# Two sliding-window attention layers between Fourier layers, on one core: exponents and scores take turns in five PSUM banks

## The chip, the cores and the metric

The kernel runs on one core of a Trainium2 chip. The metric is the device time of one execution in microseconds (us). A core has five engines with a queue each: TensorE (PE, with its weight loads shown as PEld), VectorE (DVE), ScalarE (ACT), GpSimd (POOL) and SyncE (SP), which here only issues DMAs. An engine works through its queue in order; it waits on semaphores for the others.

## The reference

```python
def _A_ref(x, wqkv, wo):                      # x: 1 x 2048 x 576
    H = 32; Dh = D // H; W = 256              # 32 heads of 18
    q, k, v = ...                             # from x @ wqkv
    scores = einsum("bhqd,bhkd->bhqk", q, k) * (Dh ** -0.5)
    mask = (0 <= idx[:, None] - idx[None, :]) & (idx[:, None] - idx[None, :] < W)
    p = softmax(where(mask, scores, -1e9))
    return einsum("bhqk,bhkd->bhqd", p, v) ... @ wo

x = A_x
x = x + _A_ref(layernorm(x), A_wqkv, A_wo)
x = x + _B_ref(layernorm(x), B_w_r, B_w_i)    # rfft2, times weights, irfft2
x = x + _A_ref(layernorm(x), A_wqkv, A_wo)
x = x + _B_ref(layernorm(x), B_w_r, B_w_i)
```

The change is in `_A_ref`, which is run twice.

## The kernel before

The program is written as one order of instructions by hand; each engine gets its instructions in that order. `layer_a` normalises and transposes the 2048 tokens, projects v, and then does attention; `layer_b` follows. All of this happens twice ("the first and the second layer" below).

Attention goes by *units*. A unit t is one tile of 128 tokens for four heads: there are 8 groups of four heads (`NQ`) and 16 tiles (`NT`), so 128 units (`NX`). The four heads are two pairs; the heads of a pair lie in the upper and lower 64 rows of the array, `hp` 0 and 1, and their matmuls run side by side.

For each unit there are two kinds of scores:

- `score_max` (S, L790 and L792) runs ten units ahead (`LEAD`). PE multiplies q by k for one tile of queries and up to 384 keys into a PSUM tile `S`; VectorE adds the mask and takes the maximum of each row into `m`. After four units, `m_rows` (L798 to L805) transposes the maxima on PE (`tpm`), ScalarE negates them (`mt`), and four DMAs on SyncE put them as a row into `qs`, so that the second multiplication subtracts them.
- `exps` (E, L822 and L823) multiplies the other way round, keys by up to 384 queries, into a PSUM tile `E`; ScalarE writes the exponent of it into `P` in SBUF, which has five buffers, one a unit. GpSimd masks `P`.

`pv` (U, L842) multiplies the exponents of the two or three tiles that matter with v, two units later, and adds up in the bank `U`. Every fourth unit ScalarE copies the sums out (`us`, L847), and `norm` transposes them (`tpo`, L852) and divides on VectorE.

Between these stand the projections to q and k (`proj`, `pj`, L741): 28 blocks of 14 steps for the groups of heads that come later, a few steps in each unit by the table `goal`. When a block's last step is done, ScalarE copies one half's sum into a buffer `sg` (L747), VectorE adds the other half (L748), GpSimd splits the result into two parts (L749, L750), and SyncE stores it into `qk_d` in DRAM (L755). `stack_load` (L769) fetches it back into `qs` and `ks`. The buffer `sg` has two copies. Units -10 to -1 have no E and no U, only S and projections; five blocks end there.

PSUM has eight banks. One is `U`, two are `pj`, three are the tag `S` (scores for maxima, `tpm`, `tpo`), and two are the tag `E` (scores for exponents). In units 118 to 123, which have no S, the second pair's E take the tag `S`. A tile of a tag with n banks waits until the reader of the tile n before it in that tag is done.

The body of a unit, in the order in which it is written:

```python
for pair in range(2):
    for hp in range(2):
        if 0 <= t < NX:
            exps(t, pair, hp)
    for hp in range(2):
        if t + LEAD < NX:
            score_max(t + LEAD, pair, hp)
    if pair == 0 and 0 <= t - 2 < NX:
        pv(t - 2)
    ...                       # for t < 2: half of the unit's projection steps
for f in more:                # the projection steps, then m_rows or norm if due
    f()
```

So PE's queue in a unit reads E E, S S, U, E E, S S, projections, and in two of four units a transposition.

Of the kernel before, what the change touches and what calls it, by code (L numbers as in the profile page):

```python
# [8 lines left out]
F32 = mybir.dt.float32  # L9
F32R = mybir.dt.float32r  # L10
# [5 lines left out]
S, D = 2048, 576  # L16
# [564 lines left out]
def layer_a(tc, src, dst, wqk_d, wv_d, wo_d, dc_d, gc_d, dram, copy, wvs, second, spectral):  # L581
    nc = tc.nc
    V, A, T, P = nc.vector, nc.scalar, nc.tensor, nc.gpsimd
    SC = float(DH) ** -0.5
    qk_d = dram.tile([2, 1152, S], F32R, name="qk_d")
# [5 lines left out]
    with ExitStack() as ctx:  # L591
# [115 lines left out]
        with ExitStack() as c2:  # L707
            wp = c2.enter_context(tc.tile_pool(name="a2", bufs=2))
            pp = c2.enter_context(tc.tile_pool(name="a2p", bufs=2, space=PSUM))
# [16 lines left out]
            def proj(i, c, tag, halves=False):  # L726

                box = {}
                ks = k_steps()
                cs = slice(c * 512, c * 512 + 512)  # L730
                parts = [slice(0, 64), slice(64, 128)] if halves else [slice(0, 128)]

                def mm(s, k):
                    wk, p, xk = k
                    if s == 7 and c == 2 and 0 < i < 8:
                        w_split(i + 1)
                    if s == 0:
                        box["ps"] = [pp.tile([128, 512], F32, tag=tag, name=f"pj{i}_{c}_{b}", bufs=2) for b in range(len(parts))]
                    w = wt[i][0] if p == "h" else wt[i][1]
                    for ps, r in zip(box["ps"], parts):  # L740
                        T.matmul(ps, w[r, wk], xT(xk, cs)[r], start=s == 0, stop=s == len(ks) - 1)  # L741
                    if s == len(ks) - 1:
                        ps = box["ps"]
                        sg = wp.tile([128, 2, 512], F32R, tag="sg", name=f"sg{i}_{c}", bufs=2)
                        if halves:
                            su = sg[:, 1].bitcast(F32)
                            A.copy(su, ps[0])  # L747
                            V.tensor_add(su, su, ps[1])  # L748
                            P.tensor_copy(sg[:, 0], su)  # L749
                            P.tensor_sub(sg[:, 1], su, sg[:, 0].bitcast(F32))  # L750
                        else:
                            A.copy(sg[:, 0], ps[0])
                            V.tensor_sub(sg[:, 1], ps[0], sg[:, 0].bitcast(F32))

                        (nc.scalar if i < 2 else nc.sync).dma_start(qk_d[:, 128 * i:128 * i + 128, cs].rearrange("a r t -> r a t").bitcast(F32), sg.bitcast(F32))  # L755
                return [lambda s=s, k=k: mm(s, k) for s, k in enumerate(ks)]

            vts = {}

# [19 lines left out]
            def score_max(x, pair, hp):  # L779

                n, i = divmod(x, NT)
                c, t = divmod(i, 4)
                q, k = qs[n % 2], ks_[n % 2]
                if t == hp == pair == 0:
                    ms[n, c] = wp.tile([128, 2, 2, 4], F32, tag="m", name=f"m{n}_{c}", bufs=3)
                lo, hi = max(0, i - 2) * 128, (i + 1) * 128
                N = hi - lo
                b = 64 * hp
                ps = pp.tile([128, 512], F32, tag="S", name=f"S{x}_{pair}_{hp}", bufs=3)
                T.matmul(ps[:, 0:N], q[b:b + 63, pair, i * 128:i * 128 + 128], k[b:b + 63, pair, lo:hi], start=True, stop=True)  # L790
                jk = wp.tile([128, 384], BF, tag="jk", name=f"jk{x}_{pair}_{hp}", bufs=3)
                V.tensor_tensor_reduce(out=jk[:, 0:N], in0=ps[:, 0:N], in1=mask[:, 384 - N:384], scale=1.0, scalar=-3e38,  # L792
                                       op0=ALU.add, op1=ALU.max, accum_out=ms[n, c][:, hp, pair, t:t + 1])

            def m_rows(n, c):
                q = qs[n % 2]
                tp = pp.tile([128, 4, 128], F32, tag="S", name=f"tpm{n}_{c}", bufs=3)
                T.transpose(tp[0:16, 0], ms[n, c].rearrange("p a b t -> p (a b t)"), ident)  # L798
                mt = wp.tile([16, 128], F32R, tag="mt", name=f"mt{n}_{c}", bufs=2)
                A.activation(mt, tp[0:16, 0], AF.Copy, scale=-1.0)  # L800
                for hp in range(2):
                    for pair in range(2):
                        r = (hp * 2 + pair) * 4
                        b = 64 * hp + 63
                        nc.sync.dma_start(q[b:b + 1, pair, c * 512:c * 512 + 512].rearrange("a (t q) -> a t q", t=4).bitcast(F32),  # L805
                                          mt[r:r + 4].bitcast(F32))
# [3 lines left out]
            def exps(x, pair, hp):  # L810

                n, j = divmod(x, NT)
                q, k = qs[n % 2], ks_[n % 2]
                nq = min(3, NT - j) * 128
                hl_ = 2 * hp + pair
                if hp == pair == 0:
                    pt[n, j] = wp.tile([128, 4, 384], F32, tag="P", name=f"P{n}_{j}", bufs=5)
                p = pt[n, j]

                ps = pp.tile([128, 512], F32, name=f"E{x}_{hl_}", **(dict(tag="S", bufs=3) if pair and NX - LEAD <= x < NX - 4 else dict(tag="E", bufs=2)))  # L820
                b = 64 * hp
                T.matmul(ps[:, 0:nq], k[b:b + 64, pair, j * 128:j * 128 + 128], q[b:b + 64, pair, j * 128:j * 128 + nq], start=True, stop=True)  # L822
                A.activation(p[:, hl_, 0:nq], ps[:, 0:nq], AF.Exp, scale=SC)  # L823
                if hp == pair == 1:
                    P.affine_select(out=p[:, :, 0:128], in_=p[:, :, 0:128], pattern=[[0, 4], [1, 128]], compare_op=ALU.is_ge,  # L825
                                    fill=0.0, base=0, channel_multiplier=-1)
                    if nq == 384:
                        P.affine_select(out=p[:, :, 256:384], in_=p[:, :, 256:384], pattern=[[0, 4], [-1, 128]], compare_op=ALU.is_gt,  # L828
                                        fill=0.0, base=0, channel_multiplier=1)
# [17 lines left out]
                    A.copy(u, U)  # L847

            def norm(n, c):
                tp = pp.tile([128, 4, 128], F32, tag="S", name=f"tpo{n}_{c}", bufs=3)  # L850
                for a in range(4):
                    T.transpose(tp[:, a], us[n, c][:, a * 128:a * 128 + 128], ident)  # L852
                tv = tp.rearrange("p a (h e) -> p (a h) e", e=32)
                rc = wp.tile([128, 16, 1], F32, tag="rc", name=f"rc{n}_{c}", bufs=2)
                V.reciprocal(rc, tv[:, :, 18:19])
                o = wp.tile([128, 4, 72], F32, tag="o", name=f"o{n}_{c}", bufs=2)
                V.tensor_mul(o.rearrange("p a (h e) -> p (a h) e", e=18), tv[:, :, 0:18], rc.to_broadcast([128, 16, 18]))
                lo, hi = 72 * n, 72 * n + 72
                for a, f0, f1 in ((o_d, 0, 448), (o7_d, 448, 576)):
                    b, e = max(lo, f0), min(hi, f1)  # L860
                    if b < e:
                        nc.sync.dma_start(a[c * 512:(c + 1) * 512, b - f0:e - f0].rearrange("(a p) e -> p a e", a=4), o[:, :, b - lo:e - lo])
# [10 lines left out]
            NX = NQ * NT  # L873
            LEAD = 10
# [4 lines left out]
            for m in range(22):  # L879
                a, b = [2 + 23 * z // 5 for z in (m, m + 1)]  # L880
# [6 lines left out]
            for t in range(-LEAD, NX + 2):  # L887
# [3 lines left out]
                n, c = divmod(t + 20, NT)  # L891
# [10 lines left out]
# [4 lines that stand above are left out]
                    for hp in range(2):  # L906
                        if t + LEAD < NX:
                            score_max(t + LEAD, pair, hp)
                    if pair == 0 and 0 <= t - 2 < NX:
                        pv(t - 2)  # L910
                    if pair == 0 and t < 2:
                        for f in more[:(len(more) + 1) // 2]:
                            f()
                        more = more[(len(more) + 1) // 2:]
                for f in more:
                    f()
                if copy and t >= 32 and t % 4 == 0 and t < 32 + 16 * len(copy):

                    z, r = divmod(t // 4 - 8, 4)
# [36 lines left out]
            for k in range(4):  # L956
                tp = pp.tile([128, 512], F32, tag="E" if k in (1, 2) else "pj", name=f"tpz{k}", bufs=2)[0:32]
# [9 lines left out]
            tp = pp.tile([128, 512], F32, tag="pj", name="tpl", bufs=2)  # L967
# [47 lines left out]
```

## Time and profile before

| | us |
|---|---|
| median of 3 runs | 1584.82 (1583.24 to 1590.53) |
| the profiled execution, and its span | 1586.13, 1584.4 |
| PE, DVE, ACT, POOL busy in the span | 1452.4, 944.0, 823.8, 753.4 |
| exponents on ScalarE (L823), 1024 times | 427.8 |
| maxima on VectorE (L792), 1024 times | 499.5 |
| attention's units -10 to 127, first layer | 106.8 to 511.7 |
| the same, second layer | 898.6 to 1303.0 |

The profile is of one execution. A row of the time line has a start, a length, the engine, the line, the tile written and the tile read, the shape, and a count where equal rows were put together; in square brackets stands the idle time before it and who ended it. Matmuls overlap and their lengths include their way through the array, so on PE the distance from start to start is the measure, not the length.

### The profile page before, as it was taken

The numbers are of one execution on the slowest core, as the hardware profiler recorded it, in microseconds if no ns is written. First come the engines' busy times: TensorE is split into PE (matmuls) and PEld (weight loads), VectorE is DVE, ScalarE is ACT, GpSimd is POOL, SyncE is SP. The second block draws the span as 40 slices with busy tenths as digits, with TensorE's granted clock in tenths as the row PEclk, the third lists the DMA queues.
The fourth block names the chain that finished last, engine by engine and source line by source line (L and its number), as shares of the span: only waits on it lengthen the run. The fifth ranks groups of instructions, "written<-read, shape, count | busy, mean of one in ns | idle before, by whom it ended". The sixth has DMA issues, their size and how long they took to land. (4 is left out here: it accounts for less than half of the span.)

```text
span 1584.4 us, 35203 instructions
## 1 busy us (share of the span) xinstructions
PE 1452.4 (92%) x12312; PEld 1077.3 (68%) x12312; DVE 944.0 (60%) x3083; ACT 823.8 (52%) x1900; POOL 753.4 (48%) x1240
## 2 busy tenths in 40 slices
PE   7998999999999899877879989999999998997787
PEld 7976666666655799536779766666666557995376
DVE  4337777777764555444543377777777645554445
ACT  5524666666667344224445246666666673442244
POOL 2185556555545333144611855555555463332445
PEclk9999999999988999988989999999999899999889
DMA  6656455554444366666474564544444443657664
GB/s 205 177 182 207 142 156 183 152 165 145 151 128 123 118 196 200 220 195 209 142 229 118 181 202 146 155 150 145 139 130 149 128 129 118 196 194 230 191 206 139
DMA packets 196414, 264.43 MB, mean 167 GB/s; under 512 B 87182, under 2 KB 109326, under 8 KB 195406
## 3 DMA queue, kind: packets, MB, share of 16 engines
q1 hardware_dynamic: 184494, 243.28, 49.6%
q10 hardware_dynamic: 10976, 15.59, 3.0%
q0 software_dynamic: 768, 3.31, 0.8%
q8 instruction: 99, 1.62, 0.4%
q14 instruction: 77, 0.63, 0.1%
HBM read 163.46 MB, written 100.91 MB: 167 GB/s over the span
## 5 line engine op out<-in xcount | busy, mean ns | idle before, releaser
L792 DVE CUSTOM_DVE_ANT_0 jk<-S,mask 128x384 bf16<-128x384 f32 (+2 forms) x1024 | 499.5, 529 | 144.3 <-PE S L790 130.8
L823 ACT ACTIVATE P<-E 128x384 f32<-128x384 f32 (+2 forms) x1024 | 427.8, 473 | 204.3 <-PE E L822 176.6
L825 POOL TENSOR_SCALAR_AFFINE_SELECT P<-P 128x512 f32<-128x512 f32 x256 | 163.0, 637 | 311.0 <-ACT P L823 292.0
L822 PE MATMUL E<-qs,ks 64*128 64x384 f32 (+2 forms) x1024 | 285.2, 429 | 10.2 <-ACT P L823 8.2
L790 PE MATMUL S<-ks,qs 63*128 63x384 f32 (+2 forms) x1024 | 250.7, 362 | 9.4 <-DVE m L792 9.0
L822 PEld LDWEIGHTS E<-qs,ks 64*128 64x128 f32 x1024 | 138.3, 186 | 136.4 <-ACT P L823 80.7
L842 PE MATMUL U<-P,vq 128*19 128x128 f32 (+1 forms) x3840 | 208.2, 336 | 0.3
L741 PE MATMUL pj<-xh,wqh 64*128 64x512 f32 (+1 forms) x640 | 172.5, 404 | 5.5 <-ACT sg L747 3.4
L790 PEld LDWEIGHTS S<-ks,qs 63*128 63x128 f32 x1024 | 141.9, 190 | 27.0 <-DVE m L792 20.5
L842 PEld LDWEIGHTS U<-P,vq 128*19 128x19 f32 x3840 | 91.2, 99 | 100.5 <-issue 40.8
L828 POOL TENSOR_SCALAR_AFFINE_SELECT P<-P 128x512 f32<-128x512 f32 x224 | 142.7, 637 | 0.0
L741 PE MATMUL pj<-xl,wqh 64*128 64x512 f32 (+1 forms) x512 | 136.1, 395 | 0.0
L741 PE MATMUL pj<-xh,wql 64*128 64x512 f32 (+1 forms) x640 | 129.2, 398 | 1.4 <-POOL wql L431 1.4
L527 PE MATMUL ops<-oroom 128*128 128x288 f32 x784 | 112.4, 299 | 4.4 <-DVE oroom L510 3.0
L527 PEld LDWEIGHTS ops<-oroom 128*128 128x128 f32 x784 | 105.2, 188 | 6.2 <-DVE oroom L510 4.0
L741 PEld LDWEIGHTS pj<-xh,wqh 64*128 64x128 f32 (+1 forms) x640 | 95.0, 187 | 11.2 <-ACT sg L747 3.9
L171 POOL TENSOR_TENSOR eo<-xn 128x287 f32<-128x287 f32 x32 | 26.1, 817 | 150.4 <-ACT xn L169 150.4
L741 PEld LDWEIGHTS pj<-xh,wql 64*128 64x128 f32 (+1 forms) x640 | 84.4, 190 | 6.9 <-POOL wql L431 2.0
L792 DVE DVE_READ_ACCUMULATOR2_ANT m<- 128x1 f32 x1024 | 85.0, 83 | 0.0
L199 PE MATMUL pf<-dc,et 128*128 128x290 f32 x384 | 72.3, 313 | 9.7 <-DVE et L190 6.5
L741 PEld LDWEIGHTS pj<-xl,wqh 64*128 64x128 f32 (+1 forms) x512 | 78.6, 187 | 3.0
L750 POOL TENSOR_TENSOR sg<-sg 128x512 fp32r<-128x512 f32 x56 | 72.2, 1289 | 4.7
(179 smaller groups left out, 2567.0 us busy)
## 6 DMA issues: line engine op xcount, KB each, us to landing
qk_d<-sg SPq DMA_DIRECT2D x56, 512.0 KB
qs<-qk_d SPq DMA_DIRECT2D x384, 72.0 KB
ks<-qk_d SPq DMA_DIRECT2D x384, 72.0 KB
v_d<-vt SPq DMA_DIRECT2D x32, 304.0 KB
vq<-v_d SPq DMA_DIRECT2D x16, 608.0 KB
yd<-ye SPq DMA_DIRECT2D x32, 290.0 KB
wt<-in_w SPq DMA_DIRECT2D x16, 580.0 KB
x<-ofree SPq DMA_DIRECT2D x32, 288.0 KB
```

Source lines behind the costliest of these rows:

```text
L171: P.tensor_add(eo[:, 0, 1:288], xn[:, 1:288], xn[:, 575:288:-1])
L199: T.matmul(o, et[:, c, si], m(5 * c + mi), start=q == 0, stop=False)
L527: self.nc.tensor.matmul(self.ps[u][n][:, 0:288], x, self.w[p][:, wk * D + n * 288:wk * D + n * 288 + 288], start=first and i == 0, stop=la ...
L741: T.matmul(ps, w[r, wk], xT(xk, cs)[r], start=s == 0, stop=s == len(ks) - 1)
L750: P.tensor_sub(sg[:, 1], su, sg[:, 0].bitcast(F32))
L790: T.matmul(ps[:, 0:N], q[b:b + 63, pair, i * 128:i * 128 + 128], k[b:b + 63, pair, lo:hi], start=True, stop=True)
L792: V.tensor_tensor_reduce(out=jk[:, 0:N], in0=ps[:, 0:N], in1=mask[:, 384 - N:384], scale=1.0, scalar=-3e38, op0=ALU.add, op1=ALU.max, accu ...
L822: T.matmul(ps[:, 0:nq], k[b:b + 64, pair, j * 128:j * 128 + 128], q[b:b + 64, pair, j * 128:j * 128 + nq], start=True, stop=True)
L823: A.activation(p[:, hl_, 0:nq], ps[:, 0:nq], AF.Exp, scale=SC)
L825: P.affine_select(out=p[:, :, 0:128], in_=p[:, :, 0:128], pattern=[[0, 4], [1, 128]], compare_op=ALU.is_ge, fill=0.0, base=0, channel_mult ...
L828: P.affine_select(out=p[:, :, 256:384], in_=p[:, :, 256:384], pattern=[[0, 4], [-1, 128]], compare_op=ALU.is_gt, fill=0.0, base=0, channel ...
L842: T.matmul(U[32 * h:32 * h + 19, (q0 % 4) * 128:(q0 % 4) * 128 + 128 * (q1 - q0)], vts[n][:, j, h], pt[n, j][:, h, (q0 - j) * 128:(q1 - j) ...
```

## The change

It has three parts. First, `bank` gives out the five banks of the tags `S` and `E` in one turn, S S E E S, to every score, exponent and transposition from unit 0 on, whichever kind it is. Second, the blocks of projections that end before unit 0 take their store buffer from the five buffers of `P` instead of the two of `sg`. Third, for these blocks only ScalarE's copy is written at once; the add, the split and the store (`rest`) are written behind the next pair of maxima.

```diff
                     if s == len(ks) - 1:
                         ps = box["ps"]
-                        sg = wp.tile([128, 2, 512], F32R, tag="sg", name=f"sg{i}_{c}", bufs=2)
-                        if halves:
-                            su = sg[:, 1].bitcast(F32)
-                            A.copy(su, ps[0])
-                            V.tensor_add(su, su, ps[1])
-                            P.tensor_copy(sg[:, 0], su)
-                            P.tensor_sub(sg[:, 1], su, sg[:, 0].bitcast(F32))
+                        if halves and t < 0:
+                            sg = wp.tile([128, 4, 384], F32, tag="P", name=f"sg{i}_{c}", bufs=5)...
                         else:
-                            A.copy(sg[:, 0], ps[0])
-                            V.tensor_sub(sg[:, 1], ps[0], sg[:, 0].bitcast(F32))
-                        (nc.scalar if i < 2 else nc.sync).dma_start(qk_d[...], sg.bitcast(F32))
+                            sg = wp.tile([128, 2, 512], F32R, tag="sg", name=f"sg{i}_{c}", bufs=2)
+                        su = sg[:, 1].bitcast(F32) if halves else ps[0]
+                        A.copy(su if halves else sg[:, 0], ps[0])
+
+                        def rest():
+                            if halves:
+                                V.tensor_add(su, su, ps[1])
+                                P.tensor_copy(sg[:, 0], su)
+                            (P if halves else V).tensor_sub(sg[:, 1], su, sg[:, 0].bitcast(F32))
+                            (nc.scalar if i < 2 else nc.sync).dma_start(qk_d[...], sg.bitcast(F32))
+                        if halves and t < 0:
+                            later.append(rest)
+                        else:
+                            rest()
+            turns, later = [0], []
+
+            def bank(name):
+                turns[0] += t >= 0
+                return pp.tile([128, 512], F32, name=name, **(dict(tag="E", bufs=2) if turns[0] % 5 > 2 else dict(tag="S", bufs=3)))

                 # score_max
-                ps = pp.tile([128, 512], F32, tag="S", name=f"S{x}_{pair}_{hp}", bufs=3)
+                ps = bank(f"S{x}_{pair}_{hp}")
                 # m_rows (and norm likewise)
-                tp = pp.tile([128, 4, 128], F32, tag="S", name=f"tpm{n}_{c}", bufs=3)
+                tp = bank(f"tpm{n}_{c}").rearrange("p (a t) -> p a t", a=4)
                 # exps
-                ps = pp.tile([128, 512], F32, name=f"E{x}_{hl_}", **(dict(tag="S", bufs=3) if pair and NX - LEAD <= x < NX - 4 else dict(tag="E", bufs=2)))
+                ps = bank(f"E{x}_{hl_}")

                     for hp in range(2):
                         if t + LEAD < NX:
                             score_max(t + LEAD, pair, hp)
+                    while later:
+                        later.pop()()
```

On PE the instructions keep their places; what they wait for changes. Here is unit 41, which follows projections, before; `E41_0` and `E41_2` are the first pair's two heads, `S51_0_0` and `S51_0_1` the maxima ten units ahead, and the word in brackets is the engine waited for.

```order
L822 MATMUL E41_0_3916<-qs0_1034,ks0_1035 128x384 [waits Activation_49]
L822 MATMUL E41_2_3919<-qs0_1034,ks0_1035 128x384 [waits Activation_49]
L790 MATMUL S51_0_0_3922<-ks1_1037,qs1_1036 128x384 [waits DVE_49]
L790 MATMUL S51_0_1_3926<-ks1_1037,qs1_1036 128x384 [waits DVE_49]
L842 MATMUL U_1038<-P2_6_3740,vq2_2748 19x256 [waits Pool_49]
```

And the same place after:

```order
L834 MATMUL E41_0_3916<-qs0_1034,ks0_1035 128x384 [waits DVE_49]
L834 MATMUL E41_2_3919<-qs0_1034,ks0_1035 128x384 [waits Activation_49]
L802 MATMUL S51_0_0_3922<-ks1_1037,qs1_1036 128x384 [waits Activation_49]
L802 MATMUL S51_0_1_3926<-ks1_1037,qs1_1036 128x384 [waits DVE_49]
L854 MATMUL U_1038<-P2_6_3740,vq2_2748 19x256 [waits Pool_49]
```

Before, both E wait for ScalarE and both S for VectorE. After, the first E waits for VectorE and the first S for ScalarE. Counted back five banks, `E41_0` takes the bank of the second maximum of the pair before the last, `E41_2` that of the last pair's first exponent, `S51_0_0` that of its second exponent, and `S51_0_1` that of its first maximum. Behind a transposition, which takes a turn too, E E S S mostly take the banks of E E S S before it, as they did.

On SyncE, ahead of unit 0, the loads for chunks 2 and 3 of the first group (L769), the stores of projections (L755) and the rows of maxima (L805) stand so before:

```order
L769 DMA qs0_1034<-qk_d_69 18x2x512 x6
L769 DMA ks0_1035<-qk_d_69 18x2x512 x6
L755 DMA qk_d_69<-sg2_0_1331 128x2x512
L769 DMA qs0_1034<-qk_d_69 18x2x512 x6
L769 DMA ks0_1035<-qk_d_69 18x2x512 x6
L755 DMA qk_d_69<-sg2_1_1403 128x2x512
...
L755 DMA qk_d_69<-sg2_3_1568 128x2x512
L755 DMA qk_d_69<-sg3_0_1629 128x2x512
L805 DMA qs0_1034<-mt0_1_1637 1x4x128 x4
```

And after:

```order
L781 DMA qs0_1034<-qk_d_69 18x2x512 x6
L781 DMA ks0_1035<-qk_d_69 18x2x512 x6
L756 DMA qk_d_69<-sg2_0_1331 128x2x512
L756 DMA qk_d_69<-sg2_1_1403 128x2x512
...
L756 DMA qk_d_69<-sg2_3_1568 128x2x512
L817 DMA qs0_1034<-mt0_1_1633 1x4x128 x4
L756 DMA qk_d_69<-sg3_0_1629 128x2x512
```

The first store moved behind the loads of the next chunk, and the fifth behind the second rows of maxima. On VectorE, the add of each of these blocks stands one pair of maxima later.

More of the change, by code (lines that the diff above doesn't have):

```diff
@@ L743, in mm @@
                         ps = box["ps"]
-                        sg = wp.tile([128, 2, 512], F32R, tag="sg", name=f"sg{i}_{c}", bufs=2)
-                        if halves:
-                            su = sg[:, 1].bitcast(F32)
-                            A.copy(su, ps[0])
-                            V.tensor_add(su, su, ps[1])
-                            P.tensor_copy(sg[:, 0], su)
-                            P.tensor_sub(sg[:, 1], su, sg[:, 0].bitcast(F32))
-                        else:
-                            A.copy(sg[:, 0], ps[0])
-                            V.tensor_sub(sg[:, 1], ps[0], sg[:, 0].bitcast(F32))
-                        (nc.scalar if i < 2 else nc.sync).dma_start(qk_d[:, 128 * i:128 * i + 128, cs].rearrange("a r t -> r a t").bitcast(F32), sg.bitcast(F32))
+                        if halves and t < 0:
+                            sg = wp.tile([128, 4, 384], F32, tag="P", name=f"sg{i}_{c}", bufs=5).rearrange("p a b -> p (a b)")[:, 0:1024].bitcast(F32R).rearrange("p (a t) -> p a t", a=2)
+                        else:
+                            sg = wp.tile([128, 2, 512], F32R, tag="sg", name=f"sg{i}_{c}", bufs=2)
[6 more added lines that the diff above has]
+                            (P if halves else V).tensor_sub(sg[:, 1], su, sg[:, 0].bitcast(F32))
+                            (nc.scalar if i < 2 else nc.sync).dma_start(qk_d[:, 128 * i:128 * i + 128, cs].rearrange("a r t -> r a t").bitcast(F32), sg.bitcast(F32))
+                        if halves and t < 0:
+                            later.append(rest)
+                        else:
+                            rest()
                 return [lambda s=s, k=k: mm(s, k) for s, k in enumerate(ks)]
+            turns, later = [0], []
+            def bank(name):
+                turns[0] += t >= 0
+                return pp.tile([128, 512], F32, name=name, **(dict(tag="E", bufs=2) if turns[0] % 5 > 2 else dict(tag="S", bufs=3)))
             vts = {}
@@ L849, in norm @@
             def norm(n, c):
-                tp = pp.tile([128, 4, 128], F32, tag="S", name=f"tpo{n}_{c}", bufs=3)
+                tp = bank(f"tpo{n}_{c}").rearrange("p (a t) -> p a t", a=4)
                 for a in range(4):
```

## The prediction

> **What bounds the kernel now.** I read the stages first (the table of windows), then who keeps TensorE waiting, then its rows in order of time, and last the rows of the engines that release it. The table's columns are time, busy time of PE, PEld, DVE, ACT and POOL, granted clock, DMA share and GB/s.
>
> ```profile
> 106.00:139.00 33.00, 26.47 (x195) 21.66 (x195) 21.47 (x83) 4.57 (x9) 21.95 (x24) 0.95 0.69 220
> 139.00:410.00 271.00, 270.02 (x2760) 170.92 (x2756) 206.14 (x799) 182.19 (x438) 158.62 (x233) 1.00 0.53 161
> ```
>
> These are the two stages that the change touches in the first layer; the second layer repeats them. From 106 to 139 us come ten units of maxima and projections, from 139 on the units proper. There PE looks full, VectorE stands at 206 of 271 us (76%) and ScalarE at 182 (67%). But the busy time of matmuls overlaps, so the waits are to be looked for where a weight load (PEld) waits. Over both layers, the weight loads of E waited this long for the exponents, with the number of times behind it:
>
> ```profile
>   ACT P L823: 88.9, 336
> ```
>
> How one such wait costs time is seen in a few rows of PE (start, length, operation):
>
> ```profile
> 232.74 0.45 PE L822 MATMUL E<-qs,ks 64*128 64x384 f32 x2
> 233.02 0.33 PE L790 MATMUL S<-ks,qs 63*128 63x384 f32 x2
> 233.28 0.85 PE L842 MATMUL U<-P,vq 128*19 128x256 f32 x16
> 234.06 0.52 PE L822 MATMUL E<-qs,ks 64*128 64x384 f32 x2
> 234.35 0.41 PE L790 MATMUL S<-ks,qs 63*128 63x384 f32 x2
> 234.52 0.93 PE L741 MATMUL pj<-xh,wql 64*128 64x512 f32 x6
> 235.23 0.68 PE L822 MATMUL E<-qs,ks 64*128 64x384 f32 x2
> 235.47 0.61 PE L790 MATMUL S<-ks,qs 63*128 63x384 f32 x2
> 236.01 0.85 PE L842 MATMUL U<-P,vq 128*19 128x256 f32 x16
> ```
>
> A unit is E E, S S, U, E E, S S, then projection steps. The unit at 232.74 came behind a transposition and has no wait: E to S 0.28, S to U 0.26, so U comes 0.54 after E. The next one, straight behind projections, has U 0.78 after E (236.01 - 235.23). Its second E began late, which its row's length shows (0.68 against 0.45). Released was it by ScalarE, whose pairs of exponents stand here:
>
> ```profile
> 234.54 0.87 ACT L823 ACTIVATE P<-E 128x384 f32<-128x384 f32 x2 [0.45 <-PE E L822]
> 235.66 0.87 ACT L823 ACTIVATE P<-E 128x384 f32<-128x384 f32 x2 [0.24 <-PE E L822]
> ```
>
> The pair that started at 234.54 ended at 235.41, and 0.06 later, at 235.47, PE went on. With two banks the second E of a pair waits for the second exponent of the pair before. Behind a copy of sums or projections on ScalarE the same wait is longer, U 0.93 after E (265.46 - 264.53):
>
> ```profile
> 264.53 0.82 PE L822 MATMUL E<-qs,ks 64*128 64x384 f32 x2
> 264.91 0.62 PE L790 MATMUL S<-ks,qs 63*128 63x384 f32 x2
> 265.46 0.85 PE L842 MATMUL U<-P,vq 128*19 128x256 f32 x16
> 263.99 0.87 ACT L823 ACTIVATE P<-E 128x384 f32<-128x384 f32 x2 [0.96 <-PE E L822]
> ```
>
> Of every four units one follows a transposition of maxima and one of sums; the other two, like these, wait. Units 2 to 117 have scores of both kinds, so 58 or 59 a layer wait, 118 in all.
>
> **The change part by part.** No arithmetic is added or removed; what moves is which release each instruction waits for.
>
> *Five banks in turn.* In an ordinary unit the first E now waits for the maximum of an S pair further back, the second E for the first exponent of the pair before, the first S for the second exponent, and the second S for a maximum, as before. So the wait for the second exponent does not go. It moves from the second E to the first S. At 235.23 both E could have run, 0.17 together where their weights lie ready:
>
> ```profile
> 374.28 0.45 PE L822 MATMUL E<-qs,ks 64*128 64x384 f32 x2
> 374.45 0.61 PE L790 MATMUL S<-ks,qs 63*128 63x384 f32 x2
> 374.99 0.85 PE L842 MATMUL U<-P,vq 128*19 128x256 f32 x16
> ```
>
> The S pair would then start at 235.47, released as the E was before. Behind a pair that had not waited U comes 0.26 later (233.28 - 233.02); for a pair that waited I add 0.11, the difference between an E pair whose weights could not be loaded ahead and one whose could (0.28 - 0.17). U would stand at 235.84 instead of 236.01: 0.17 saved. For the longer wait the exponent ended at 264.86, S at 264.91, U at 264.91 + 0.37 = 265.28 instead of 265.46: 0.18. Some units save nothing: at 374.28 the E pair ran through and S waited, for a maximum, which the change leaves. Ends: 0 a unit, if U stays where it is, and 0.78 - (0.17 + 0.26) = 0.35 or more, if the wait went whole. I take 0.18 for 118 units, nearest to the two cases worked out: **-21 us**.
>
> What is late next is VectorE. The second S waits for the maximum of the S before:
>
> ```profile
> 234.72 0.56 DVE L792 CUSTOM_DVE_ANT_0 jk<-S,mask 128x384 bf16<-128x384 f32 x1 [0.17 <-PE S L790]
> 235.20 0.08 DVE L792 DVE_READ_ACCUMULATOR2_ANT m<- 128x1 f32 x1
> ```
>
> It was ready at 235.28, 0.19 before the release at 235.47; that is the cover under which this part stands.
>
> *The last units* (124 to 127) have no scores and now use two banks alone, at 503.60 and 504.62:
>
> ```profile
> 503.60 0.69 PE L822 MATMUL E<-qs,ks 64*128 64x384 f32 x2
> 504.62 0.82 PE L822 MATMUL E<-qs,ks 64*128 64x384 f32 x2 [0.33 <-ACT P L823]
> ```
>
> Five in turn let E run ahead, but ScalarE (0.87 a pair) then sets the pace. Ends 0 and 0.33 for eight pairs, 2.6 a layer; I take 1 a layer, since the first exponents are the only ones to come sooner: **-2 us**.
>
> *The first units.* Two buffers hold the projections until their store has landed; the third copy waited 6.14 us for it, and PE stood behind VectorE's queue:
>
> ```profile
> 130.85 0.59 ACT L747 COPY sg<-pj 128x512 f32<-128x512 f32 x1 [6.14 <-DMA qk_d<-sg]
> 125.96 0.44 PE L790 MATMUL S<-ks,qs 63*128 63x384 f32 x1 [2.42 <-DVE m L792]
> 137.23 0.50 PE L741 MATMUL pj<-xh,wqh 64*128 64x512 f32 x1 [1.54 <-ACT sg L747]
> ```
>
> With the exponents' five buffers no copy of these five tiles waits for a store, and the add stands behind the next maxima instead of ahead of them. PE would be at unit 0 earlier by at least 2.42 + 1.54 = 4.0. But unit 2 (E at 143.62) needs the second four rows of maxima, and these SyncE issues in turn:
>
> ```profile
> 116.63 2.75 SPq L769 DMA_DIRECT2D ks<-qk_d  x6
> 120.29 0.38 SPq L755 DMA_DIRECT2D qk_d<-sg  x1
> 120.72 2.71 SPq L769 DMA_DIRECT2D qs<-qk_d  x6
> 123.47 2.54 SPq L769 DMA_DIRECT2D ks<-qk_d  x6
> 126.21 0.38 SPq L755 DMA_DIRECT2D qk_d<-sg  x1
> 138.33 2.01 SPq L755 DMA_DIRECT2D qk_d<-sg  x2
> 140.43 2.65 SPq L805 DMA_DIRECT2D qs<-mt  x4
> 143.62 0.75 PE L822 MATMUL E<-qs,ks 64*128 64x384 f32 x2
> ```
>
> The last of them is issued at 143.08, half a microsecond before unit 2's E. The queue is nearly closed; what opens is the wait ahead of the first store (120.29 - 119.38 = 0.91), 0.20 ahead of the second, 2.01 - 2 x 0.38 = 1.25 between the last two, and one store of 0.38 that now stands behind the rows: 2.7 us a layer. Units 0 to 4 get their exponents' buffers only when the five stores have landed. A store takes 4.6 us (issued at 126.21, and the copy of 130.85 waited for it). The fifth is now issued behind the rows, at 143.08 - 2.7 = 140.4, and lands at 145.0; unit 4, two units of 2.5 (232.74 to 235.23) behind a unit 2 at 140.9, wants its buffer at 145.9. So I cost it at nothing, with 0.9 of cover, and at 2 us a layer if the store lands late. Ends: a gain of 4.0 and a loss of 2 a layer. PE will now idle longer just before unit 2, so I take 2 of the 2.7: **-4 us**.
>
> *Sum*: -21 - 2 - 4 = -27. The profiled execution took 1586.1 us, 1.3 over the median of 1584.8; that gives 1559 for it and **1558** for the median.
>
> **The rivals.** *The whole wait goes* (12%). If the pair never meets the second exponent, 0.35 to 0.50 is saved 118 times, 50 us with 0.42 each, and 4 a layer at the front: about 1585 - 50 - 8 - 2 = 1525. For it speaks that the engines have room (76% and 67%); against it that the first S hangs on that same exponent.
>
> *The wait only moves* (15%): the S pair meets it and its own late weights, U comes no sooner, and 6 us at the ends are left: 1579. For it speaks the row at 374.45, where a late S cost as much as a late E: U 0.54 behind.
>
> *Exponents wait for maxima: slower* (5%). E now hangs on VectorE, the busiest of the three readers. If its copies and sums push maxima back past E's turn, ScalarE, the masks and U are late in turn. It decides where the maximum comes more than 0.19 + 0.18 later against the exponents than in the rows above. A loss of 0.2 in 118 units is 24 us: 1608. Against it: the first E takes a maximum ahead of the two rows of VectorE above, so one that was over by 234.72, half a microsecond before that E at 235.23.
>
> *The clock* (3%). It was halved in these units:
>
> ```profile
> 443.00:464.00 21.00, 18.99 (x181) 10.11 (x181) 15.76 (x62) 14.73 (x36) 12.26 (x18) 1.00 0.60 184
> 464.00:485.00 21.00, 20.48 (x133) 10.52 (x133) 12.51 (x47) 10.99 (x29) 9.81 (x13) 0.51 0.05 9
> ```
>
> In the same 21 us VectorE did 47 instructions against 62, a quarter less. If another 160 us ran so, 40 us would be lost: 1598. The stage that already cycles through two and three banks shows 1.00. The Trainium skill, "TensorE: Matmul & The Clock Gate", section "A second HAM failure mode: psum-queue depth-cycling", says that going round the banks leaves small idle times in which the clock falls back again and again. By that rule the new turn would not help; the trace bears it out in no stage with projections.
>
> **How the numbers follow.** The forecast has 65% (1546 to 1570, from 0.10 to 0.28 a unit). With the others at 12, 15, 5 and 3, the range that leaves out the whole wait's end and both slower cases, 20%, reaches from 1538 to 1580. A half percent, 8 us, is about what a measurement of this kernel can tell; the case in which the wait only moves lies at that border and is split. Faster 0.85, same 0.08, slower 0.07.
>
> **What would show it.** Right: in units behind projections E and S 0.17 apart, S waiting for ScalarE, U 0.60 to 0.75 after E; the wait of E's weight loads for exponents well under half of 88.9 us; no copy waiting for a store ahead of unit 0; unit 2's E 2 to 3 us sooner after the stage's start. Wrong: U as late after E as before, E waiting for maxima in large numbers, or a granted clock under 0.95 from 139 to 410 us.

## The result and the profile after

The changed kernel took 1566.85 us (median of 4 runs, 1565.35 to 1572.51) against 1584.03 of the kernel before on the same chip: ratio 0.9894, 95% interval 0.9852 to 0.9936. That is 17 us less, where 26 to 27 were forecast; 1566.85 lies in the range of 1538 to 1580. The profiled execution took 1565.98, its span 1564.3 (before: 1584.4). In a second measurement the ratio was 0.9854 (0.9799 to 0.9909).

The table of stages of the changed kernel, with the columns as before (time, busy PE, PEld, DVE, ACT, POOL, granted clock, DMA share, GB/s):

```profile
106.00:139.00 33.00, 29.77 (x231) 23.56 (x229) 26.52 (x103) 8.54 (x18) 24.85 (x28) 1.00 0.67 217
139.00:410.00 271.00, 265.51 (x2786) 168.68 (x2786) 206.16 (x799) 181.67 (x439) 158.73 (x234) 0.99 0.54 164
```

PE did more in the first stage (231 rows against 195), because its waits there are shorter. In the second it lost nearly 5 us at one place, of which more below. What E waits for (three lines of the view of its line, now L834; us, times, weight loads and matmuls together):

```profile
  ACT P L835: 28.9, 94
  DVE m L804: 12.8, 52
  DMA qs<-mt: 12.0, 3
```

and of S, after (now L802) and then before (L790):

```profile
  DVE m L804: 21.2, 69
  ACT P L835: 16.8, 85
```

```profile
  DVE m L792: 29.5, 53
  issue: 0.9, 3
```

E's wait for exponents fell from 88.9 to 28.9, and S, which did not wait for exponents before, now does, 16.8. New at E are a wait for maxima, and one for the rows of maxima, which come by DMA. An ordinary unit straight behind projections, on PE and ScalarE:

```profile
233.93 0.33 PE L834 MATMUL E<-qs,ks 64*128 64x384 f32 x2
234.17 0.44 PE L802 MATMUL S<-ks,qs 63*128 63x384 f32 x2
234.54 0.85 PE L854 MATMUL U<-P,vq 128*19 128x256 f32 x16
233.24 0.87 ACT L835 ACTIVATE P<-E 128x384 f32<-128x384 f32 x2 [0.46 <-PE E L834]
```

Both E run through (0.33 long). S starts at 234.17, 0.06 behind the end of ScalarE's pair (233.24 + 0.87 = 234.11): the first S now has the wait that the second E had. U comes 0.61 after E; it was 0.78. That is the step the prediction worked out. But not every unit has it:

```profile
237.07 0.44 PE L834 MATMUL E<-qs,ks 64*128 64x384 f32 x1
237.74 0.44 PE L834 MATMUL E<-qs,ks 64*128 64x384 f32 x1 [0.23 <-ACT P L835]
236.69 0.60 ACT L749 COPY sg<-pj 128x512 f32<-128x512 f32 x1
237.16 1.68 ACT L835 ACTIVATE P<-E 128x384 f32<-128x384 f32 x4
```

Here ScalarE had a copy of a projection ahead of its exponents. The second E of a unit's second half waits, in a turn of five, for the first exponent of the same unit, which ran from 237.16 to 237.69 (it is the first of the four that the last row puts together). Where ScalarE is that far behind, E waits as before.

The first units went otherwise than forecast. ScalarE's row of maxima for unit 2, SyncE's queue, and PE at unit 2:

```profile
130.27 0.26 ACT L812 ACTIVATE mt<-tpm 16x128 fp32r<-16x128 f32 x1
126.39 1.19 SPq L609 DMA_DIRECT2D wqr<-in_wqk  x1
127.68 2.92 SPq L817 DMA_DIRECT2D qs<-mt  x4
130.64 0.44 SPq L786 DMA_DIRECT2D vq<-v_d  x1
131.19 0.38 SPq L756 DMA_DIRECT2D qk_d<-sg  x1
131.61 3.03 SPq L781 DMA_DIRECT2D qs<-qk_d  x6
135.52 4.13 SPq L781 DMA_DIRECT2D ks<-qk_d  x6
139.75 0.39 SPq L756 DMA_DIRECT2D qk_d<-sg  x1
140.23 2.54 SPq L817 DMA_DIRECT2D qs<-mt  x4
142.99 1.00 PE L834 MATMUL E<-qs,ks 64*128 64x384 f32 x2 [4.79 <-DMA qs<-mt]
143.00:147.00 4.00, 4.00 (x16) 2.98 (x16) 2.09 (x8) 1.75 (x4) 1.23 (x2) 0.50 0.63 195
```

The rows of maxima for unit 2 were ready on ScalarE at 130.53 and were issued only at 140.23. Before, they were ready later and issued at about the same time, 140.43:

```profile
137.07 0.26 ACT L800 ACTIVATE mt<-tpm 16x128 fp32r<-16x128 f32 x1
```

PE came to unit 0 some 6 to 7 us sooner, stood 4.79 ahead of unit 2, and ran at half clock to about 147 (last row of the first view). In the second layer it stood 6.91.

I count a stage from its first S, and a unit from its first exponent. Units 2 to 104 then took 295.2 and 294.9 us in the two layers, against 301.4 and 301.0; but unit 2 itself came at 36.7 and 38.9, against 37.4 and 38.7.

### The profile page after: what moved, and what is told of

Read it like the earlier page. It is cut to its first block, busy times and chain, and to the rows that moved or that the text cites. A ratio compares the mean times of both kernels' runs of the same rounds, so it can differ in the third digit from the quotient of the medians.

```text
span 1564.3 us, 35449 instructions
## 1 busy us (share of the span) xinstructions
PE 1427.6 (91%) x12312; PEld 1066.9 (68%) x12312; DVE 943.4 (60%) x3083; ACT 819.4 (52%) x1900; POOL 753.5 (48%) x1240
## 3 DMA queue, kind: packets, MB, share of 16 engines
q8 instruction: 99, 1.62, 0.4%
## 5 line engine op out<-in xcount | busy, mean ns | idle before, releaser
L834 PE MATMUL E<-qs,ks 64*128 64x384 f32 (+2 forms) x1024 | 237.9, 416 | 18.3 <-DMA qs<-mt 12.0
L802 PE MATMUL S<-ks,qs 63*128 63x384 f32 (+2 forms) x1024 | 233.2, 367 | 3.0 <-DVE m L804 1.9
L834 PEld LDWEIGHTS E<-qs,ks 64*128 64x128 f32 x1024 | 119.7, 186 | 109.5 <-issue 55.6
L741 PE MATMUL pj<-xh,wqh 64*128 64x512 f32 (+1 forms) x640 | 165.3, 405 | 4.3 <-DVE sg L753 2.6
L802 PEld LDWEIGHTS S<-ks,qs 63*128 63x128 f32 x1024 | 130.4, 188 | 41.7 <-DVE m L804 19.2
L741 PE MATMUL pj<-xl,wqh 64*128 64x512 f32 (+1 forms) x512 | 127.6, 395 | 0.0
L741 PE MATMUL pj<-xh,wql 64*128 64x512 f32 (+1 forms) x640 | 120.8, 393 | 1.1 <-POOL wql L431 1.1
L741 PEld LDWEIGHTS pj<-xh,wqh 64*128 64x128 f32 (+1 forms) x640 | 87.0, 188 | 9.9 <-DVE sg L753 3.3
L741 PEld LDWEIGHTS pj<-xh,wql 64*128 64x128 f32 (+1 forms) x640 | 71.8, 186 | 9.7 <-POOL wql L431 1.8
L755 POOL TENSOR_TENSOR sg<-sg 128x512 fp32r<-128x512 f32 x56 | 72.1, 1288 | 4.7
L741 PEld LDWEIGHTS pj<-xl,wqh 64*128 64x128 f32 (+1 forms) x512 | 70.5, 189 | 3.8
```

Of the source, the lines that this page charges most:

```text
L755: (P if halves else V).tensor_sub(sg[:, 1], su, sg[:, 0].bitcast(F32))
```

## The experiments

Twelve runs followed, one of them the changed kernel again. Times are medians; ratios are to the kernel before on the same chip, with their 95% interval. A chip's own level differs by some us, so the ratios, or kernels of one group, are compared.

**The two parts apart.** *turns_only* has the turn alone:

```diff
-                        if halves and t < 0:
+                        if False:
                             sg = wp.tile([128, 4, 384], F32, tag="P", ...
...
-                        if halves and t < 0:
+                        if False:
                             later.append(rest)
```

> The five banks in turn alone; the first units' projections are stored and summed as before. My theory after the two traces: ordinary units give about 0.13 us each (7 us a layer), the last units 1 each, and the part for the first units gave nothing, because unit 2 waits for the rows of maxima behind a load in SyncE's queue. Then this kernel takes as long as the changed one, 1564 to 1570 us. Rival: the first units' part is worth its forecast 2 a layer; then 1569 to 1575. Second rival: the earlier start pays for most of it; then over 1575.

*front_only* has the other part alone:

```diff
-    return pp.tile(..., **(dict(tag="E", bufs=2) if turns[0] % 5 > 2 else dict(tag="S", bufs=3)))
+    return pp.tile(..., **(dict(tag="E", bufs=2) if name[0] == "E" and not last else dict(tag="S", bufs=3)))
```

> The first units' part alone (projections' sums in the exponents' buffers, stored from there, summed behind the next maxima); exponents and scores in two and three banks as before. My theory: unit 0 starts some 6 us sooner, unit 2 at the same time as before after 5 to 7 us of waiting, and the clock falls behind that wait: 1582 to 1588, no gain. Rival, by the forecast's term: 4 us less than before, 1578 to 1581.

Measured: turns_only 1566.92, ratio 0.9849 (0.9820 to 0.9879); front_only 1586.06, ratio 0.9992 (0.9966 to 1.0018). The turn alone gives all that the change gives; the first units' part alone gives nothing. In front_only unit 0 came at 27.0 and 26.8 (before 32.8 and 33.7), unit 2 at 37.3 and 38.0 (before 37.4 and 38.7).

**What holds unit 2.** The load at 131.61 to 139.65 belongs to the next head group, and stands ahead of the rows. In *late_load* it stands behind them:

```diff
-                n, c = divmod(t + 20, NT)
+                n, c = divmod(t + 17, NT)
                 if c % 4 == 0 and 0 < n < NQ:
                     stack_load(n, c // 4)
```

> The changed kernel with each group of loads for the maxima (24 DMAs of q and k) issued three units later, so that in SyncE's queue the second rows of maxima stand ahead of the first such load of the next head group instead of behind it. My theory (SyncE's queue sets unit 2): unit 2's exponents start 4 to 6 us sooner after the stage's start, the wait for rows (12.0 us in all) falls under 3 and the half clock behind it goes: 5 to 7 us a layer, 1552 to 1558. Rival: the landing of the fifth store, or VectorE's maxima, holds unit 2 or 3 instead: 1562 to 1568.

The same edit on the kernel before:

> The kernel before with the same three units' delay of these loads. My theory: before, the copies that wait for stores and PE's unit 0 hold the first units about as far back as the queue does, so moving the load alone gives 0 to 2 us: 1581 to 1585. Rival: the queue alone held unit 2 there, then 3 us a layer or more: under 1579.

Measured: late_load 1593.87, ratio 1.0032 (1.0015 to 1.0049); before_late_load 1626.26, ratio 1.0252 (1.0216 to 1.0289). Both forecasts of the time were wrong, and yet the theory was right at its place: unit 2 came at 31.7 and 32.1, with no wait for rows, and unit 16 at 73.0 and 72.6 where the changed kernel had 78.6 and 80.4. The time was lost later, in places like this:

```profile
181.04 2.48 SPq L781 DMA_DIRECT2D qs<-qk_d  x6
183.57 3.40 SPq L781 DMA_DIRECT2D ks<-qk_d  x6
187.07 2.88 SPq L817 DMA_DIRECT2D qs<-mt  x4
189.62 0.41 PE L834 MATMUL E<-qs,ks 64*128 64x384 f32 x1 [3.49 <-DMA qs<-mt]
```

Where a transposition of maxima is put off by one unit (the loop lets none be issued in a unit that ends a projection), a load delayed by three units now stands directly ahead of its rows. E waited for rows 29.5 us in all, 8 times. In before_late_load unit 2 came at 37.9 and 40.1, no sooner than before: there PE itself was late (unit 0 at 33.3 and 34.3, against 27.2 and 26.8 in late_load). So unit 2 had two bounds at nearly the same time, the front of PE's queue and SyncE's; undoing one shows the other.

Four units instead of three avoid that place. *late4*, and beside it the changed kernel again:

```diff
-                n, c = divmod(t + 20, NT)
+                n, c = divmod(t + 16, NT)
```

> The changed kernel with the loads of q and k for the maxima issued four units later instead of three: ahead of unit 2 the second rows of maxima still pass the first load of the next head group, and at the other group borders no load stands directly ahead of rows that are held back one unit (where three units made PE wait eight times). My theory: unit 2's exponents come at about 32 after the stage's first S instead of 36.7 to 38.9 and that lead of 5 to 7 us a layer stays to the end: 1552 to 1560. Rival: the lead is lost again in the following units to the loads that now come later, 1564 or more.

> The changed kernel once more, on the same chip as the three others, as the measure for them. Ratio to the kernel before 0.985 to 0.992.

Measured: late4 1553.33, ratio 0.9809 (0.9759 to 0.9859); after_again 1561.97, ratio 0.9854 (0.9799 to 0.9909). In late4 SyncE and PE at unit 2:

```profile
133.19 3.99 SPq L817 DMA_DIRECT2D qs<-mt  x4
137.28 0.39 SPq L756 DMA_DIRECT2D qk_d<-sg  x1
137.71 3.54 SPq L781 DMA_DIRECT2D qs<-qk_d  x6
139.16 0.50 PE L834 MATMUL E<-qs,ks 64*128 64x384 f32 x2
139.00:410.00 271.00, 269.52 (x2815) 170.10 (x2813) 209.19 (x810) 184.18 (x446) 161.07 (x239) 1.00 0.53 162
```

The rows are issued at 133.19 instead of 140.23, E waits for rows 0.2 us in the whole run (12.0 before this edit), and PE is busy 269.5 of 271 us at clock 1.00 (265.5 at 0.99). Unit 2 came at 32.0 and 32.9, unit 104 at 328.5 and 328.2, against 331.3 and 331.8 in after_again: of the 4.6 to 4.7 us gained at unit 2, 2.9 and 3.6 are kept.

**Which release the scores need.** *e3s2_4* is late4 with three banks for exponents alone and two for scores and transpositions, instead of five in turn:

```diff
-    ... tag="E", bufs=2) if turns[0] % 5 > 2 else ... tag="S", bufs=3 ...
+    ... tag="E", bufs=2) if t >= 0 and name[0] != "E" else ... tag="S", bufs=3 ...
```

> As the kernel with the load four units later, but not five banks in turn: from unit 0 on the exponents have three banks of their own and the scores (with the transpositions) two. An exponent's matmul then waits for exponents only, 0.44 earlier ones than with two banks; a score waits for the maximum two scores back. My theory (maxima are ready only 0.2 us ahead of the exponents' release, so that scores need the third bank): the first scores of a unit wait for the maxima of the pair right before, U comes 0.2 to 0.4 later in every second unit, 12 to 24 us a layer: 24 to 48 us slower than the kernel with the turn. Rival (ScalarE's release is the only bound): 0.1 to 0.2 less in 118 units, 12 to 24 us faster than it.

Measured: 1683.9, ratio 1.0554 (1.0469 to 1.0639). The sign is that of my theory, but the size is some 118 us against late4 by the two ratios (0.0745 of 1580.45), where 24 to 48 were expected. In the traces units 4 to 104 took 334.0 and 331.7 us against 290.7 and 288.5, which is 86 us in both layers. The units behind projections and behind transpositions of maxima account for 48 of these, as the theory had it; the other 38 I had not thought of. Behind a transposition of sums, which takes one of the two banks, PE reads:

```profile
252.10 0.44 PE L834 MATMUL E<-qs,ks 64*128 64x384 f32 x2
252.39 0.33 PE L802 MATMUL S<-ks,qs 63*128 63x384 f32 x1
253.11 0.41 PE L802 MATMUL S<-ks,qs 63*128 63x384 f32 x1 [0.39 <-DVE o L869]
253.45 0.85 PE L854 MATMUL U<-P,vq 128*19 128x256 f32 x16
```

The second S waits until VectorE has normalised the sums (o), and U comes 1.35 after E; with five banks such a unit has 0.55 (231.99 - 231.44 in the changed kernel). Over the run S waits for maxima 222 times, 63.4 us, against 69 times, 20.5 in late4. So with two banks VectorE's releases are on the path, and it is the turn of five that keeps most of them off it. A further 48 us were lost in units 104 to 127, where the granted clock was 0.50 from 495 to 540 and 0.51 from 1345 to 1390.

*defer_all4* is late4 with all sums of projections behind the next maxima:

```diff
-                        if halves and t < 0:
+                        if halves:
                             later.append(rest)
```

> As the kernel with the load four units later, and the sums of all projections, not only of those ahead of unit 0, stand behind the next pair of maxima. Theory: in the changed kernel the second pair of scores waits for maxima behind such a sum (0.30 to 0.42 where 0.18 is the least) in about 12 of 28 such units a layer: 2 to 3 us a layer less. Rival: the next projection waits for its two banks, which the later sum still holds, and the time rises by 0.3 us or more in each of 23 units, 7 us a layer or more.

Measured: 1562.51, ratio 0.9861 (0.9807 to 0.9916); late4 had 0.9809 (0.9759 to 0.9859). Units 4 to 104 took 291.5 and 291.0 against 290.7 and 288.5. There is no gain; whether the 9 us of the medians are a loss, the intervals leave open.

**The half clock at the end of the stage.** The executions differ most in units 108 to 118: 25 to 35 us a layer in the kernels so far, and 41 and 43 in e3s2_4. In late4's second layer it looked like this (ScalarE, PE, then the table of stages):

```profile
1227.14 0.67 ACT L478 CAST oroom<-ofree 128x576 fp32r<-128x576 f32 x1 [1.82 <-DMA ofree<-in_wo]
1228.26 0.69 PE L834 MATMUL E<-qs,ks 64*128 64x384 f32 x1 [1.30 <-ACT P L835]
1227.00:1247.00 20.00, 18.48 (x113) 9.87 (x113) 11.25 (x43) 11.54 (x30) 9.12 (x11) 0.57 0.21 59
```

ScalarE's first copy of the output weights (L478, unit 108) waits for their load, with the exponents behind it; E waits for the exponents; in this wait, from 1227.8 on, the clock is halved, for some 17 us. Units 108 to 118, against the wait ahead of that copy: 0 to 0.6 us of wait, 26 to 27 us (four layers of after, after_again, turns_only and late4); 0.89 to 1.82 us, 30 to 35 us (ten layers of these, before, front_only and defer_all4). late_load and before_late_load have no wait there and 25 to 27 us; their half clock stands in units 104 to 108, behind waits for rows. e3s2_4 does not fit: no copy waits for its load there, and yet the clock is halved in both layers. The edit puts all five copies two units later:

```diff
-                if 0 <= t - (OB - 12) < 10 and (t - (OB - 12)) % 2 == 0:
-                    out.split((t - (OB - 12)) // 2)
+                if 0 <= t - (OB - 10) < 10 and (t - (OB - 10)) % 2 == 0:
+                    out.split((t - (OB - 10)) // 2)
```

> As the kernel with the load four units later, and ScalarE's five copies of output weights stand two units later each (units 110 to 118 instead of 108 to 116). In the traces so far ScalarE waited for these weights ahead of the first copy, and where it waited 0.89 us or more, TensorE's clock was halved behind it for 8 to 20 us and units 108 to 118 took 30 to 34 us; where it waited 0.6 or less, they took 26 to 27. My theory: that wait is what halves the clock there. Then it is gone in both layers, units 108 to 118 take 26 to 28, and the time is 1544 to 1549, against 1553 without it. Rival: the clock falls because ScalarE, not TensorE, sets the pace when the projections are done; then it is halved as often as before and the time stays at 1550 to 1556.

> The changed kernel with only the copies of output weights two units later. With the same kernel before it gives the change's own worth without that half clock. My theory: 1553 to 1559, as layer 0 of both its traces lost 4 to 7 us there. Rival as above: 1560 to 1567.

> The kernel before with only the copies of output weights two units later. My theory: both layers of its trace lost 6 to 8 us to the half clock, so 1570 to 1576; the changed kernel with the same edit then stands 15 to 20 below it, the turn's worth of 7 to 8 a layer in units 4 to 104 and 1 a layer behind. Rival as above: 1580 to 1588. Second rival (part of the change's gain was luck with the clock): the difference between the two falls to 10 or less.

The fourth of the group has late4_wo's two edits on the kernel with the turn alone:

> The first of these kernels with the first units' part undone: projections ahead of unit 0 use two buffers and their sums stand ahead of the next maxima. My theory: with the queue open that part is worth its 4 us a layer (the waits of 2.42 and 1.54 us of TensorE that it removes): 7 to 9 us slower than with it, 1551 to 1558. Rival: the rows of maxima come no later without it, and the two take the same time within 2 us.

| kernel | us | ratio | unit 2, two layers | units 108 to 118 |
|---|---|---|---|---|
| before_wo | 1579.41 | 0.9956 (0.9934 to 0.9977) | 37.8, 39.3 | 27.3, 27.3 |
| after_wo | 1558.99 | 0.9821 (0.9793 to 0.9849) | 37.9, 36.9 | 25.7, 25.7 |
| late4_wo | 1549.43 | 0.9757 (0.9732 to 0.9783) | 31.6, 33.6 | 26.0, 26.1 |
| turns_late4_wo | 1561.25 | 0.9836 (0.9809 to 0.9864) | 38.6, 38.3 | 26.0, 26.0 |

The stretch of 440 to 490 us, of the kernel before and of before_wo:

```profile
440.00:490.00 50.00, 47.07 (x392) 24.75 (x391) 33.93 (x135) 31.21 (x77) 26.23 (x37) 0.80 0.32 93
440.00:490.00 50.00, 46.24 (x462) 24.95 (x466) 35.20 (x141) 36.52 (x90) 30.25 (x43) 1.00 0.32 94
```

In all eight layers no copy waits for its load and units 108 to 118 run at full clock, as the theory has it. That the wait alone does it is not shown: the edit also puts ScalarE's work of copying later, and e3s2_4 has the half clock without that wait. The times follow less than I expected: before_wo 1579.4 (1570 to 1576), late4_wo 1549.4 (just above 1544 to 1549), after_wo 1559.0 (1553 to 1559). For the kernel before the gain is shown by its interval, 0.44%; for the other two the intervals with and without the edit (late4, after_again) overlap. after_wo stands 20.4 below before_wo, where 15 to 20 were expected, and their intervals lie far apart: the change's gain was not luck with the clock.

turns_late4_wo settles the first units' part: with the queue open it is worth 11.8 us by the medians (1561.25 - 1549.43) and 9.9 by the attention stages of the two traces, more than the 7 to 9 expected. late4_wo is the fastest kernel of the study, 2.4% below the one before.

## Why the prediction was right, and which term was not

The forecast of faster holds, and its mechanism is seen in the rows. Term by term, best read from before_wo and after_wo, which differ by the change alone and have no half clock in units 108 to 118:

- *Five banks in turn, -21.* Units 4 to 104 took 295.3 and 295.3 before, 287.4 and 287.5 after; units 104 to 118 38.7 and 38.8 against 37.2 and 37.2. Together -18.9, or 0.16 for each of the 118 units instead of 0.18. The rows show where it comes from: in the 104 units behind projections among units 4 to 103 of both layers the second pair's E comes 1.62 behind the first's in before_wo and 1.47 in after_wo (means), and behind transpositions 1.33 to 1.35 in both. 0.15 in 104 units is 15.7, all that units 4 to 104 gained. Right, by the wait moved and not removed: the rival in which the wait goes whole (1525) would have been 50 us. The cover of 0.19 for the second S held in most units: in the first two traces S waits for maxima 69 times, 21.2 us in all (before: 53 times, 29.5).
- *The last units, -2.* Units 118 to 127 took 19.4 and 19.7, then 18.4 and 18.4: -2.3. The term was for units 124 to 127, and these gave -1.4 (7.6 and 7.9, then 7.1 and 7.1); the rest lies in units 118 to 123, which it did not count. The size is right, in part by luck.
- *The first units, -4.* This is the term that failed: unit 4 came 1.2 later in one layer and 1.0 sooner in the other, so nothing. The failed step is "what opens is the wait ahead of the first store [...]: 2.7 us a layer". The waits ahead of the stores did go (the first two stores were issued at 125.41 in the changed kernel, the second at 126.21 before), and no copy ahead of unit 0 waits for a store any more. But behind them a load of weights took 1.19 instead of 0.41, and the next head group's load took 8.0 us in all instead of 7.0. In that load the waits for other DMAs to land were there before too (0.9 and 1.1, before 0.7 and 1.1); those for loads of q grew, to 2.3 us from 120 to 150 us against 1.0. So unit 2's rows were issued 0.2 sooner. I had added up the waits that would go and not asked, for every load in that queue, what it would wait for next. late4_wo against turns_late4_wo shows that PE's side of the step was right and worth more than I gave it once the queue is open. (The row of 6.14 us that the prediction shows is the fourth copy's; the third, at 124.13, waited 2.83. And its 88.9 us are waits of E's weight loads and matmuls together, 80.7 of them the weight loads'. And 0.10 a unit makes 1567, not 1570. None of this changes a term.)
- *Exponents wait for maxima* (5%): 12.8 us of such waits in all, 52 of them, most only 0.21 long and in units behind projections. It did not decide. e3s2_4 shows how near it is: with two banks for VectorE's readers the same kernel is slower by some 118 us, and in units 4 to 104 of the traces by 86.
- *The clock* (3%): 0.99 from 139 to 410, and 1.00 there in late4, which goes round the same five banks. The Trainium skill, "TensorE: Matmul & The Clock Gate", "A second HAM failure mode: psum-queue depth-cycling", would have the clock fall back with such cycling; with five in turn the clock fell in the units with projections only at waits in the first units and, in late_load, at waits for rows. (e3s2_4, which goes round three and two banks, has 0.97 to 0.98 from 200 to 480.) The half clock of the changed kernel stands at the wait for rows ahead of unit 2 and behind the wait for the output weights.

The sum by these two traces is -18.9 - 2.3 + 0.2 = -21.0, and the medians of the two kernels differ by 20.4. That these agree so well is in part chance: the spans of the two traces differ by 15.1 only (1572.0 and 1556.9), since stages that the change does not touch took some 6 us longer in after_wo's, most of it behind the last unit. The first comparison showed 17.2, with an interval of 10 to 23; one reason seen in its traces is that either kernel may have the half clock in either layer (both layers of before, one of after). The prediction took the range for the turn's size and had no term for that.

## What to carry to other kernels

Where an instruction waits for a buffer, write down the whole turn of buffers before and after: here a longer turn moved the wait to a later instruction, and what was saved is what could run ahead of it, not the wait. A first unit that is held by two queues at nearly the same time gave nothing here when one of them was relieved; look for the DMA that stands ahead of the needed one in the issuing queue and is needed later, and move it, but look then at every later place where the same rule sets the order. When runs of one kernel scatter by 1%, compare the traces of two runs stage by stage first: here a half clock that mostly came with a copy waiting a microsecond for a load was the largest difference.

## What the chip did that I had not expected

The clock fell at small waits. In the kernel before, no wait of PE in the rows from 459 to 464 us is longer than 0.56, and the clock was 0.51 from 464 to 485, with PE busy in 20.5 of 21 us; in late4 it fell within one wait of 1.30, and the 20 us from 1227 on had 0.57, with PE busy in 18.5. The Trainium skill, "TensorE: Matmul & The Clock Gate", "HAM oscillation — how this bites in real kernels", gives the rule that idle gaps over some 3.4 us are to be avoided. The 4.79 us at unit 2 of the changed kernel agree with it (0.50 from 143 to 147); the two places above show that shorter ones can do it too. In the kernel before, three of them stand close together there (0.41, 0.56 and 0.25). What exactly is counted there was not tried, and two things stay open: late4's first layer had 0.75 to 0.83 from 464 to 472 with a wait of only 0.23 ahead of the copy, and e3s2_4 ran at half clock for tens of microseconds with no such wait.
